# q, k and v as one long run per partition, and two small products of the attention as tiles side by side on TensorE

## The chip, the cores and the metric

The kernel runs on one core of a Trainium2 chip. TensorE multiplies, with a stationary operand of up to 128 x 128 and float32 results in PSUM; VectorE, ScalarE and GpSimd work element by element; DMA queues of SyncE (SP) and ScalarE move data between DRAM and SBUF. The metric is the device time of one execution in microseconds.

## The reference, cut to what matters

```python
def _attn_ref(q, k, v, p):                # q, k, v: 8 x 8 x 576 x 64, p: 8 x 8 x 32 x 64
    def sm_attn(qq, kk, vv):              # softmax(scale * qq kk^T) vv
        ...
    p_packed = sm_attn(p, k, v)           # p': 32 x 64 per head
    return sm_attn(q, p_packed, p_packed)

def reference(**kwargs):
    attn_out = _attn_ref(**attn_kwargs)
    x = np.ascontiguousarray(attn_out.transpose(0, 2, 1, 3)).reshape(B * S, H * D)   # 4608 x 512
    x = _moe_ref(x=x, **moe_kwargs)       # (P / Q)(x w_in) w_out, d_ff 2048
    return _moe2_ref(x=x, **moe2_kwargs)  # leaky(x w2_in) w2_out
```

The second attention ends in a product with p', and its result goes into a product with w_in. The kernel joins the two: W = p' w_in is computed once per batch (256 rows of 8 heads x 32 packed keys, 2048 columns), and the first feed-forward then multiplies the second softmax a2 with W.

## The kernel before, in words

The attention works through 16 items: item i is half a batch (4 of 8 heads), in two pairs of heads j. Eighteen units run as a software pipeline; in unit k each stage handles another item. The order inside a unit is the string `ORDER = "1AKWBwwVEWwPWQwT2WRw"`, one letter per step:

- `1` (`emit_s1`, item k): four float32 products give the scores of p and k in PSUM; VectorE takes the negated maximum `nm` (L315), ScalarE the exponential with its sum (L318).
- `T` (`emit_T`, item k-1): five transposes on TensorE (L325, L326), copied to SBUF by ScalarE and VectorE.
- `P` (`emit_PP`, item k-2): softmax times v. The 576 keys are five chunks of up to 128; each chunk is one product of 128 rows (two heads pairs x 32 packed keys, both j) with 256 columns (four heads). Of the result only the blocks of a row's own pair are used: two VectorE instructions (L344), one per half of the partitions, scale them by the sum's reciprocal and by `mask`, which zeroes the other head of the pair.
- `R` (`emit_PPT`, item k-2): p' is transposed on TensorE and copied into `pph`.
- `2` (`emit_s2`, item k-3): scores of q and p' (L361), transposed in 32 x 32 blocks by VectorE (L365), maximum (L368), subtraction on GpSimd (L369).
- `E`, `A`, `B` (items k-4, k-5): exponential on ScalarE (L372), sums, division, transpose back, and the store of a2 to DRAM, which SP issues (L389).
- `K`, `V`, `Q`: loads of k (item k+2), v (item k-1) and q (item k-2), all issued by SP; `pt`, `kt`, `vt`, `qt` are their tiles.
- `W` (`wb_step`, `emit_Wb`): one block of p' times w_in, 128 x 512, for a pair of batches bp, a pair of heads j and a quarter fc of w_in's columns; four a unit. For bp 0 `emit_Wb0` (L400) does another form, 64 x 256 products with output halves on alternating partitions, from unit 6 on; from unit 10 on `emit_Wb` (L421) runs. The stationary operand of L421 is `pph[bp][:, j]`, 128 x 128 with zeros where a head meets the other head's rows. The result lies in one of two PSUM tiles of the pool `psw`; ScalarE copies it to `wbs` (L433), in the last bp VectorE does every second one (L431). Two blocks fill a `wbs`, and `store_Wb` sends it to DRAM at the next `W`.
- `w`: one step of the work that splits float64 weights into float32 pieces, w_in until about 62 us, then half of w_out; its loads are issued by ScalarE's queue, its arithmetic stands between the attention's on ScalarE, VectorE and GpSimd.

Each engine works its list in this order, so an instruction that waits holds all behind it. After the loop the string `DRAIN` finishes the last items and ten more blocks W, the remaining six (`FILL`) stand in the first steps of the first feed-forward, which begins near 190 us.

A float32 product appears in the trace as two MATMUL records. The layout in DRAM before: q and k as [batch, pair, 128, 576], so a partition of a load gets two runs of 576 x 4 = 2304 B; v as [batch, 576, 512], so a chunk's row gives 256 x 4 = 1024 B.

## Time and profile before

| | |
|---|---|
| median of 3 runs | 1541.99 us (1541.19 to 1542.47) |
| profiled execution | 1541.61 us, its span 1539.8 us |
| TensorE (PE) busy | 1472.9 us, 96% of the span |
| VectorE (DVE) busy | 1307.6 us, 85% |
| ScalarE (ACT) busy | 1029.5 us, 67% |
| GpSimd (POOL) busy | 563.2 us, 37% |
| mean granted TensorE clock | 0.990 of 2.4 GHz |
| DMA | 322.23 MB, mean 209 GB/s |

The shares are means over stages with different limits: the attention ends near 205 us, the first feed-forward near 831 us, the second fills the rest. PEld is TensorE's loading of the stationary operand, which overlaps PE. Matmuls are pipelined, so neighbouring records overlap, and the end of a record is modelled; the chain of waits counts each stretch of time once. The DMA share is the mean busy share of 16 DMA engines; it can exceed 1 slightly.

### The profile page before, as it was taken

What the parts mean: (1) busy time and instruction counts of PE and PEld (TensorE: products, weight loads), DVE (VectorE), ACT (ScalarE), POOL (GpSimd) and SP (SyncE); (2) the same over time, 40 slices, a digit from 0 to 9 for tenths busy, and PEclk for the clock granted to TensorE, in tenths of its full rate; (3) what the DMA queues carried; (4) which work ended last, traced back from release to release, by engine and by line L of the source; (5) the groups of instructions that cost most, each with busy time, mean ns of one, the idle gap of its engine ahead of it and who ended that gap; (6) DMA issues with size and microseconds to landing.
All of it is one profiled execution on the core that took longest, in us unless ns stands there. A gap on an engine that the chain in (4) does not pass through costs nothing.

```text
span 1539.8 us, 20601 instructions
## 1 busy us (share of the span) xinstructions
PE 1472.9 (96%) x7552; PEld 1214.8 (79%) x7552; DVE 1307.6 (85%) x1428; ACT 1029.5 (67%) x1193; POOL 563.2 (37%) x338
## 2 busy tenths in 40 slices
PE   4798879999999999999999999999999999999998
PEld 2454467888888888888888877888888888888898
DVE  5989789898988998999999799968965996599586
ACT  5456488888988888888886676447534743474363
POOL 1223168788788768887664520000000000000000
PEclk9999989999999999999999999999999999999999
DMA  9798964325443533434335877997567656765694
GB/s 348 275 314 265 316 209 130 96 82 178 142 132 121 173 104 117 139 101 137 110 110 183 310 267 234 367 382 292 180 221 286 198 186 217 256 193 200 217 408 172
DMA packets 151108, 322.23 MB, mean 209 GB/s; under 512 B 14816, under 2 KB 79328, under 8 KB 149984
## 3 DMA queue, kind: packets, MB, share of 16 engines
q1 hardware_dynamic: 147552, 308.34, 58.3%
q10 hardware_dynamic: 3456, 12.58, 2.3%
q8 instruction: 60, 0.98, 0.3%
q14 instruction: 40, 0.33, 0.1%
HBM read 230.17 MB, written 90.70 MB: 208 GB/s over the span
## 4 chain that ended last, share of the span: by engine, by line
PE 55%; DVE 15%; ACT 13%; POOL 7%; issue 5%; DMA 4%; SPq 1%; ACTq 0%; POOLq 0%; DVEq 0%
PE p L1065 20%; PE p L1057 20%; PE acc L651 6%; PE h L572 4%; DVE s L91 2%; POOL s L705 2%; DMA qt<-in_qT 1%; DVE s L94 1%; DVE s L88 1%; PE pw L421 1%; PE pp L340 1%; POOL wb L522 1%; ACT h L629 1%; ACT wb L521 1%; DVE v L900 1%
## 5 line engine op out<-in xcount | busy, mean ns | idle before, releaser
L651 PE MATMUL acc<-gt,wo 128*128 128x512 f32 x1728 | 404.9, 390 | 7.0 <-ACT yo L588 7.0
L651 PEld LDWEIGHTS acc<-gt,wo 128*128 128x128 f32 x1728 | 320.1, 188 | 71.2 <-ACT yo L588 8.3
L1057 PE MATMUL p<-ysp,ws 128*128 128x512 f32 (+1 forms) x1680 | 346.9, 368 | 2.9 <-ACT vsp L985 2.4
L1065 PE MATMUL p<-vsp,ws 128*128 128x512 f32 (+1 forms) x1680 | 346.5, 368 | 0.2 <-DVE vsp L986 0.2
L1057 PEld LDWEIGHTS p<-ysp,ws 128*128 128x128 f32 x1680 | 292.5, 189 | 56.8 <-ACT vsp L985 3.4
L1065 PEld LDWEIGHTS p<-vsp,ws 128*128 128x128 f32 x1680 | 292.3, 189 | 53.7 <-DVE vsp L986 1.5
L572 PEld LDWEIGHTS h<-a2t,wb 128*128 128x128 f32 x1728 | 230.0, 194 | 30.3 <-issue 18.5
L572 PE MATMUL h<-a2t,wb 128*128 128x192 f32 (+2 forms) x1728 | 236.3, 293 | 17.3 <-DVE v__1851 L636 5.6
L985 ACT ACTIVATE vsp<-v 128x1024 fp32r<-128x1024 f32 (+1 forms) x140 | 135.7, 971 | 147.6 <-PE p L1065 98.4
L986 DVE TENSOR_TENSOR vsp<-v,vsp 128x1024 fp32r<-128x1024 f32 (+1 forms) x140 | 155.7, 1112 | 32.4 <-ACT vsp L985 31.9
L900 DVE TENSOR_TENSOR v<-v,p 128x1024 f32<-128x1024 f32 (+1 forms) x100 | 110.7, 1109 | 40.7 <-PE p L1057 40.4
L917 DVE SCALAR_TENSOR_TENSOR v<-r,nalpha,v 128x512 f32<-128x512 f32 (+1 forms) x160 | 112.3, 742 | 29.7 <-ACT v L912 29.7
L911 ACT ACTIVATE r<-v 128x1024 f32<-128x1024 f32 (+1 forms) x60 | 58.3, 972 | 76.3 <-DVE v L900 75.9
L900 DVE TENSOR_TENSOR v<-v 128x1024 f32<-128x1024 f32 (+1 forms) x80 | 88.3, 1109 | 0.0
L522 POOL TENSOR_TENSOR wb<-s,wb 128x512 fp32r<-128x512 f32 x48 | 64.7, 1348 | 31.0 <-ACT wb L521 30.5
L88 DVE TENSOR_SCALAR s<-s 128x512 f32<-128x512 f32 x48 | 63.8, 1328 | 0.6 <-ACT s L83 0.6
L912 ACT ACTIVATE v<-v 128x1024 f32<-128x1024 f32 (+1 forms) x60 | 58.6, 976 | 1.9
L91 DVE SCALAR_TENSOR_TENSOR s<-s,s 128x512 int32<-128x512 int32 x40 | 56.8, 1419 | 0.3
L925 ACT ACTIVATE v<-p 128x1024 f32<-128x1024 f32 (+1 forms) x20 | 18.9, 943 | 53.3 <-PE p L1057 53.3
L369 POOL TENSOR_TENSOR trn<-trn,mx 128x576 f32<-128x576 f32 x16 | 20.3, 1268 | 90.9 <-DVE mx L368 80.6
L900 DVE TENSOR_TENSOR c<-c,p 128x1024 f32<-128x1024 f32 (+1 forms) x25 | 27.4, 1112 | 29.9 <-PE p L1065 29.6
L421 PE MATMUL pw<-w_in,pph 128*128 128x512 f32 x96 | 48.5, 619 | 3.9 <-ACT wbs L433 3.9
(1024 smaller groups left out, 2260.6 us busy)
## 6 DMA issues: line engine op xcount, KB each, us to landing
ws<-wh_d SPq DMA_DIRECT2D x224, 512.0 KB, 5.6
wh_d<-ws SPq DMA_DIRECT2D x56, 512.0 KB, 5.0
wq_d<-s SPq DMA_DIRECT2D x32, 512.0 KB, 3.9
wst<-wq_d SPq DMA_DIRECT2D x56, 256.0 KB, 3.9
wb_d<-wbs SPq DMA_DIRECT2D x48, 256.0 KB, 4.5
s<-in_w_out SPq DMA_DIRECT2D x24, 512.0 KB, 4.4
s<-wb_d SPq DMA_DIRECT2D x48, 256.0 KB, 4.2
kt<-in_kT SPq DMA_DIRECT2D x16, 576.0 KB, 7.9
```

What stands on the lines that cost most here:

```text
L88: dve.tensor_scalar(w, w, 0.0, HIGH_R, op0=ALU.max, op1=ALU.min)
L91: dve.scalar_tensor_tensor(wi, in0=wi, scalar=3, in1=low, op0=ALU.logical_shift_left, op1=ALU.bitwise_or)
L421: mm(pw, pph[bp][:, j].rearrange("p a b -> p (a b)"), w_in_t[j, fc], start=True, stop=True)
L522: pool.tensor_tensor(t[:, 1], st, t[:, 0], op=ALU.subtract)
L572: mm(h[:, ft, o:o + m], w[x][:, k, 128 * ft:128 * ft + 128], a2_t[c][:, y, k, o:o + m], start=n == 0, stop=n == 5)
L651: mm(acc[d // 2][:, d % 2, :], w[:, x, 128 * d:128 * d + 128], t[:, y, ft, :], start=f == 0 and (x, y, ft) == (0, 0, 0), stop=f == NP - 1 ...
L900: dve.tensor_tensor(o, a, b, op=op)
L917: dve.scalar_tensor_tensor(v_[:, g], in0=r[:, g], scalar=nalpha[:, f:f + 1], in1=v_[:, g], op0=ALU.mult, op1=ALU.add)
L985: act(t[:, 0, :, 0:m], src, AF.Copy)
L986: return lambda: dve.tensor_tensor(t[:, 1, :, 0:m], src, t[:, 0, :, 0:m], op=ALU.subtract)
L1057: mm(ps[:, g, 0:m], w[:, g, x, 128 * k:128 * k + 128], ysp[s, i](z, k), start=not onto and q == 0, stop=q == 5, skip_group_check=again)
L1065: mm(ps[:, d, 0:m], w[:, g, x, 128 * d:128 * d + 128], t[:, z, g, 0:m], start=not onto and n == 0 and g == 0 and q == 0, stop=n == 3 and g ...
```

## The change

1. q and k lie in DRAM as [batch, half, 128, 2, 576]: a partition of a load is one run of 4608 B. v lies in the order of the tile: the 64 upper partitions get five chunks as one run of 5120 B, the 64 lower ones four chunks, 4096 B. The number of loads and their bytes stay.
2. Softmax times v: each chunk is two products of 64 columns of the stationary operand with 128 columns, one for each j, on output partitions 0 to 63 and 64 to 127. The result is 128 x 128 and one VectorE instruction scales and masks it; `mask` has three column blocks of 64 and is read from block 0 or 1. In pairs 1 and 2 of a batch (`TURN`) the two heads stand in turned order, which p's layout on the host sets.
3. p' times w_in: two neighbouring pairs j are computed together into two PSUM tiles by eight products of 64 rows (one head) and 32 columns (32 packed keys of one head and batch); the zero blocks are left out. The copies stay one per `W` step, in the order j0, j0+1 for a quarter of w_in's columns, then the next quarter, so two `wbs` fill at the same time.

```diff
--- before.py
+++ after.py
@@ -203,11 +203,10 @@
 
     ident = sp0.tile([128, 128], F32, tag="ident", name="ident", bufs=1)
     make_identity(nc, ident)
-    mask = sp0.tile([128, 128], F32, tag="mask", name="mask", bufs=1)
+    mask = sp0.tile([128, 3, 64], F32, tag="mask", name="mask", bufs=1)
     pool.memset(mask, 0.0)
-    for h in range(4):
-        o = 64 * (h % 2)
-        pool.memset(mask[32 * h:32 * h + 32, o:o + 64], 1.0)
+    for h, c in ((0, 0), (0, 2), (1, 1), (2, 1), (3, 0), (3, 2)):
+        pool.memset(mask[32 * h:32 * h + 32, c, :], 1.0)
 
     pt, kt, qt, vt = {}, {}, {}, {}
 
@@ -218,19 +217,18 @@
             nc.sync.dma_start(out=pt[b], in_=pT[b])
             pool.tensor_scalar(pt[b], pt[b], 0.125, None, op0=ALU.mult)
         kt[i] = sp0.tile([128, 2, S], F32, tag="kt", name="kt", bufs=3)
-        nc.sync.dma_start(out=kt[i], in_=kT[b, 2 * t:2 * t + 2].rearrange("j p s -> p j s"))
+        nc.sync.dma_start(out=kt[i], in_=kT[b, t])
 
     def load_v(i):
         b, t = divmod(i, 2)
         vt[i] = sp0.tile([128, 5, 256], F32, tag="vt", name="vt")
-        vs = v[b, :, 256 * t:256 * t + 256]
-        nc.sync.dma_start(out=vt[i][:, 0:4, :], in_=vs[0:512].rearrange("(c p) d -> p c d", p=128))
-        nc.sync.dma_start(out=vt[i][0:64, 4, :], in_=vs[512:576])
+        for r, c, x in ((0, 5, v[b, t, 0:64 * 1280]), (64, 4, v[b, t, 64 * 1280:64 * 2304])):
+            nc.sync.dma_start(out=vt[i][r:r + 64, 0:c, :], in_=x.rearrange("(p c d) -> p c d", p=64, c=c))
 
     def load_q(i):
         b, t = divmod(i, 2)
         qt[i] = sp0.tile([128, 2, S], F32, tag="qt", name="qt")
-        nc.sync.dma_start(out=qt[i], in_=qT[b, 2 * t:2 * t + 2].rearrange("j p s -> p j s"))
+        nc.sync.dma_start(out=qt[i], in_=qT[b, t])
 
     w_in_t = {}
 
@@ -333,16 +331,15 @@
     def emit_PP(i):
         pb = ps0.tile([128, 512], F32, tag="pp", name="pp")
         pps[i] = pb
-        pp = pb[:, 0:256]
+        pp = pb[:, 0:128]
         at, v_ = a1T.pop(i), vt.pop(i)
         for c in range(5):
             kc = 128 if c < 4 else 64
-            mm(pp, at[0:kc, c, :], v_[0:kc, c, :], start=c == 0, stop=c == 4)
+            for j in range(2):
+                mm(pp[64 * j:64 * j + 64, :], at[0:kc, c, 64 * j:64 * j + 64], v_[0:kc, c, 128 * j:128 * j + 128],
+                   start=c == 0, stop=c == 4)
         ppn[i] = sp0.tile([128, 128], F32, tag="ppn", name="ppn", bufs=1)
-        for j in range(2):
-            r = slice(64 * j, 64 * j + 64)
-            dve.scalar_tensor_tensor(ppn[i][r, :], in0=pp[r, 128 * j:128 * j + 128],
-                                     scalar=rs1[i][r, :], in1=mask[r, :], op0=ALU.mult, op1=ALU.mult)
+        dve.scalar_tensor_tensor(ppn[i], in0=pp, scalar=rs1[i], in1=mask[:, i % 2:i % 2 + 2, :].rearrange("p a b -> p (a b)"), op0=ALU.mult, op1=ALU.mult)
 
     def emit_PPT(i):
         b, t = divmod(i, 2)
@@ -388,7 +385,8 @@
         b, t = divmod(i, 2)
         nc.sync.dma_start(out=a2_d[b][:, t, :], in_=a2.pop(i))
 
-    wbs, stores = {}, []
+    TURN = (0, 1, 1, 0)
+    wbs, stores, pws = {}, [], {}
 
     def emit_Wb0(n):
 
@@ -409,30 +407,35 @@
         bp, r = divmod(n, 16)
         if bp == 0:
             return emit_Wb0(n)
-        j, fc = BLOCKS[r]
-        if bp == LAST and r % 4 > 1 and "ps0" in opened:
-            if fc % 2 == 0:
-                wbs[1] = ps0.tile([128, 2, 512], F32, tag="s1", name="pw")
-            pw = wbs[1][:, fc % 2, :]
-        elif bp == LAST and r % 4 > 1:
-            pw = psw2.tile([128, 512], F32, tag="wb", name="pw")
-        else:
-            pw = psw.tile([128, 512], F32, tag="wb", name="pw")
-        mm(pw, pph[bp][:, j].rearrange("p a b -> p (a b)"), w_in_t[j, fc], start=True, stop=True)
+        j0, fc = 2 * (r // 4 % 2), 2 * (r // 8) + r % 4 // 2
+        if r % 2 == 0:
+            if bp == LAST and r % 4 > 1 and "ps0" in opened:
+                two = ps0.tile([128, 2, 512], F32, tag="s1", name="pw")
+                pws[0], pws[1] = two[:, 0, :], two[:, 1, :]
+            else:
+                for x in range(2):
+                    pws[x] = (psw2 if bp == LAST and r % 4 > 1 else psw).tile([128, 512], F32, tag="wb", name="pw")
+            for q in range(4):
+                for x in range(2):
+                    bi, h = q // 2, q % 2
+                    rows, c = slice(64 * h, 64 * h + 64), 32 * (h ^ TURN[j0 + x])
+                    mm(pws[x][64 * bi + c:64 * bi + c + 32, :], pph[bp][rows, j0 + x, bi, c:c + 32],
+                       w_in_t[j0 + x, fc][rows, :], start=True, stop=True)
+        x = r % 2
         if fc % 2 == 0:
             if bp == LAST and r > 0:
-                wbs[0] = wp.tile([128, 1024], F32, tag="D", name="wbs")
-            elif bp == LAST or len(w_done) == len(w_jobs) and n % 4 == 0:
-                wbs[0] = gp.tile([128, 1024], F32, tag="s4", name="wbs", bufs=3)
+                wbs[x] = wp.tile([128, 1024], F32, tag="D", name="wbs")
+            elif bp == LAST or len(w_done) == len(w_jobs) and x == 0:
+                wbs[x] = gp.tile([128, 1024], F32, tag="s4", name="wbs", bufs=3)
             else:
-                wbs[0] = spw.tile([128, 1024], F32, tag="wbs", name="wbs")
+                wbs[x] = spw.tile([128, 1024], F32, tag="wbs", name="wbs")
         o = 512 * (fc % 2)
-        if bp == LAST and n % 2:
-            dve.tensor_copy(wbs[0][:, o:o + 512], pw)
+        if bp == LAST and x:
+            dve.tensor_copy(wbs[x][:, o:o + 512], pws[x])
         else:
-            act(wbs[0][:, o:o + 512], pw, AF.Copy)
+            act(wbs[x][:, o:o + 512], pws[x], AF.Copy)
         if fc % 2:
-            stores.append((bp, j, fc, wbs[0]))
+            stores.append((bp, j0 + x, fc, wbs[x]))
 
     def store_Wb():
         while stores:
@@ -1095,7 +1098,13 @@
     NK = p.shape[2]
 
     def pairs_T(x):
-        return np.ascontiguousarray(x.transpose(0, 1, 3, 2)).reshape(B, H // 2, 2 * D, S)
+        return np.ascontiguousarray(x.transpose(0, 1, 3, 2).reshape(B, H // 4, 2, 2 * D, S).transpose(0, 1, 3, 2, 4))
+
+    def keys_first(x):
+        x = x.reshape(B, H // 4, 4, S, D).transpose(0, 1, 3, 2, 4).reshape(B, H // 4, S, 4 * D)
+        m = x[:, :, 0:512].reshape(B, H // 4, 4, 128, 4 * D).transpose(0, 1, 3, 2, 4)
+        top = np.concatenate([m[:, :, 0:64], x[:, :, 512:576].reshape(B, H // 4, 64, 1, 4 * D)], axis=3)
+        return np.concatenate([y.reshape(B, H // 4, -1) for y in (top, m[:, :, 64:128])], axis=2)
 
     def bits(x):
         x = np.ascontiguousarray(x)
@@ -1103,11 +1112,13 @@
 
     pT = np.zeros((B, 2, D, H // 2, 2, NK), p.dtype)
     for h2 in range(2):
-        pT[:, h2, :, :, h2, :] = p[:, h2::2].transpose(0, 3, 1, 2)
+        for turn in range(2):
+            j = np.array([turn, 3 - turn])
+            pT[:, h2, :, j, h2 ^ turn, :] = p[:, 2 * j + h2].transpose(1, 0, 3, 2)
...
-        "v": np.ascontiguousarray(v.transpose(0, 2, 1, 3)).reshape(B, S, H * D),
+        "v": keys_first(v),
```

On TensorE, unit 11 of the attention (the units up to 15 are alike) was, with what each row waits for (`Activation` is ScalarE, `DVE` VectorE, `DMAHW` a landing; `ps` are the scores, `pst` the transposed softmax, `pp` softmax times v, `pw` a block of p' times w_in):

```order
L312 MATMUL ps_1081<-kt,pt 64x288 [waits DMAHW3_49,DVE_49]
L312 MATMUL ps_1081<-kt,pt 64x288 x3
L421 MATMUL pw<-w_in,pph 128x512 [waits Activation_49] x2
L340 MATMUL pp<-vt,a1T 128x256 [waits DMAHW6_49,DVE_49]
L340 MATMUL pp<-vt,a1T 128x256 x3
L340 MATMUL pp<-vt,a1T 128x256 [waits DMAHW7_49]
L421 MATMUL pw<-w_in,pph 128x512 [waits Activation_49]
L325 MATMUL pst<-ident,a_993 128x128 x4
L326 MATMUL ps_1081<-ident,a_993 64x128
L361 MATMUL ps_1155<-qt,pph 64x288 [waits DMAHW2_49]
L361 MATMUL ps_1155<-qt,pph 64x288 x3
L421 MATMUL pw<-w_in,pph 128x512 [waits Activation_49]
```

and now is:

```order
L310 MATMUL ps_1131<-kt,pt 64x288 [waits DMAHW3_49,DVE_49]
L310 MATMUL ps_1131<-kt,pt 64x288 x3
L422 MATMUL pw<-w_in,pph 32x512 [waits Activation_49]
L422 MATMUL pw<-w_in,pph 32x512 [waits PE_49,Activation_49]
L422 MATMUL pw<-w_in,pph 32x512 x6
L339 MATMUL pp<-vt,a1T 64x128 [waits DMAHW7_49,DMAHW6_49,DVE_49]
L339 MATMUL pp<-vt,a1T 64x128 x9
L422 MATMUL pw<-w_in,pph 32x512 [waits Activation_49] x2
L422 MATMUL pw<-w_in,pph 32x512 x6
L323 MATMUL pst<-ident,a_1027 128x128 x4
L324 MATMUL ps_1131<-ident,a_1027 64x128
L358 MATMUL ps_1221<-qt,pph 64x288 [waits DMAHW0_49]
```

The four blocks at four places have become two groups of eight products at the first and the third place. The first two products of each group wait for ScalarE's copies of both blocks of the group before; in the second group these copies stand on ScalarE before and behind the exponential of the second attention. No block follows the scores of q any more.

On SP, one unit of the same stretch, from the load of k to the load of q (`wb_d` is W in DRAM, `a_d` the stored a2), was:

```order
L221 DMA kt<-in_kT 128x2x576
L441 DMA wb_d_78<-wbs 64x1024
L441 DMA wb_d_79<-wbs 64x1024
L389 DMA a_d_103<-a_1093 128x576
L227 DMA vt<-in_v 128x4x256
L228 DMA vt<-in_v 64x256
L441 DMA wb_d_78<-wbs 64x1024
L441 DMA wb_d_79<-wbs 64x1024
L233 DMA qt<-in_qT 128x2x576
```

and now is:

```order
L220 DMA kt<-in_kT 128x1152
L444 DMA wb_d_78<-wbs 64x1024
L444 DMA wb_d_79<-wbs 64x1024
L386 DMA a_d_103<-a_1143 128x576
L226 DMA vt<-in_v 64x1280
L226 DMA vt<-in_v 64x1024
L231 DMA qt<-in_qT 128x1152
L444 DMA wb_d_78<-wbs 64x1024
L444 DMA wb_d_79<-wbs 64x1024
```

The load of q has moved ahead of one pair of W's stores; the loads' rows show one run per partition.

## Rows read from the trace of the kernel before

**Rows 1.** Busy time by stage: us, PE, PEld, DVE, ACT, POOL, granted clock, DMA share, GB/s
```profile
13.46:43.05 29.59, 18.58 (x80) 10.29 (x81) 23.80 (x53) 15.24 (x30) 2.85 (x3) 0.88 1.05 377
43.05:62.77 19.72, 14.55 (x65) 8.41 (x65) 16.63 (x40) 8.56 (x16) 3.68 (x2) 0.83 0.63 213
62.77:101.50 38.73, 38.73 (x259) 22.72 (x256) 35.53 (x81) 16.82 (x33) 7.72 (x7) 1.00 0.94 316
101.50:151.79 50.29, 46.21 (x200) 23.55 (x198) 44.63 (x98) 33.48 (x64) 17.60 (x15) 1.00 0.89 286
151.79:175.90 24.11, 24.11 (x94) 12.40 (x94) 18.41 (x40) 10.49 (x19) 2.95 (x3) 1.00 0.96 309
...
200.00:203.00 3.00, 1.10 (x3) 0.19 (x1) 2.93 (x5) 2.88 (x6) 0.00 (x0) 1.00 1.02 408
```

**Rows 2.** Chain of waits, first 43 us: start us, us, what
```profile
21.97 12.83 DMA qt<-in_qT
34.81 8.24 DMA qt<-in_qT
```

**Rows 3.** Chain of waits, part of a unit of the third stage
```profile
81.83 1.73 PE pw L400 x16
83.56 2.55 PE pp L340 x10
86.11 1.01 PE pw L400 x8
```

**Rows 4.** Chain of waits, a unit of the fifth stage
```profile
159.95 1.72 PE pw L421 x4
161.66 2.35 PE pp L340 x10
164.02 1.05 PE pw L421 x2
165.07 0.44 PE pst L325 x4
...
165.62 1.12 PE ps L361 x8
166.74 1.06 PE pw L421 x2
```

**Rows 5.** SP's queue, first and last of eleven loads: start us, us, issue
```profile
13.46 0.37 SPq L227 DMA_DIRECT2D vt<-in_v  x1
...
42.32 0.53 SPq L233 DMA_DIRECT2D qt<-in_qT  x1
```

**Rows 6.** Groups by line, 0 to 330 us: count, busy us, mean ns, idle before
```profile
L344 DVE SCALAR_TENSOR_TENSOR ppn<-pp,rs,mask 64x128 f32<-64x128 f32 x32 | 10.7, 334 | 2.6 <-PE pp L340 2.3
```

**Rows 7.** Timelines of VectorE, GpSimd and ScalarE, from 158.8 us: start us, us
```profile
158.83 0.85 DVE L365 STREAM_TRANSPOSE trn<-ps 128x288 f32<-128x288 f32 x2 [0.78 <-PE ps L361]
...
159.71 0.75 DVE L368 TENSOR_REDUCE mx<-trn 128x18 f32<-128x576 f32 x1
...
160.54 1.16 POOL L369 TENSOR_TENSOR trn<-trn,mx 128x576 f32<-128x576 f32 x1 [8.12 <-DVE mx L368]
...
161.73 0.68 ACT L372 ACTIVATE trn<-trn 128x576 f32<-128x576 f32 x1 [0.29 <-POOL trn L369]
162.32 0.58 ACT L433 ACTIVATE wbs<-pw 128x512 f32<-128x512 f32 x1
```

**Rows 8.** Waits, 101.5 to 151.79 us: total us, times, longest
```profile
PEld pw L421 <- ACT wbs L433: 4.6, 8, 1.5
```

**Rows 9.** Busy time of single units, columns as in rows 1
```profile
81.83:91.19 9.36, 9.36 (x67) 5.55 (x64) 8.37 (x21) 4.17 (x8) 2.01 (x3) 1.00 0.92 294
101.50:111.40 9.90, 9.90 (x43) 5.08 (x42) 8.62 (x20) 6.70 (x13) 3.29 (x3) 1.00 1.00 347
159.95:167.91 7.96, 7.96 (x33) 4.22 (x33) 6.33 (x15) 3.46 (x7) 1.16 (x1) 1.00 0.98 332
```

**Rows 10.** Timeline of GpSimd at the start
```profile
4.04 0.85 POOL L219 TENSOR_SCALAR pt<-pt 128x256 f32<-128x256 f32 x1 [1.81 <-DMA pt<-in_pT]
```

More of the change, by code (lines that the diff above doesn't have):

```diff
@@ L36, in attention_then_two_moes @@
     B = qT.shape[0]
-    S = qT.shape[3]
+    S = qT.shape[4]
     HS = S // 2
```

## The prediction

> **What bounds the kernel now.** I read the busy times by stage first, then the chain of waits inside each stage that the change touches, then single instructions for the prices. All edits lie in the attention part, which ends near 205 us. The stages behind it contain none of the edited lines; they can only start earlier or later.
>
> By stage [rows 1] the attention part has four different limits. From 13.46 to 43.05 us the DMA engines are full: share 1.05, 377 GB/s. The chain says the same [rows 2]: it hangs on landings of q of 12.83 and 8.24 us. From 43.05 to 62.77 us the DMA share falls to 0.63 and VectorE holds 16.63 of 19.72 us. From 62.77 to 101.50 us TensorE has no gap (38.73 of 38.73), with VectorE close behind (35.53) and DMA at 0.94. From 101.50 to 151.79 us VectorE (44.63 of 50.29) and ScalarE pass the work to each other, while TensorE is only nearly full. From 151.79 to 175.90 us TensorE is again without a gap and VectorE falls to 18.41.
>
> In a unit of the third stage the product of softmax and v takes 2.55 of 9.36 us [rows 3, 9]. In one of the fifth [rows 4] it takes 2.35 and the four blocks of p' times w_in take 1.72 + 1.05 + 1.06 = 3.83 of 7.96 us, all on the chain; that unit's VectorE is busy for 6.33 us [rows 9].
>
> **The change part by part.** The sum is made against the profiled execution, 1541.61 us; the median of the runs is 0.4 us above it.
>
> *Layout of q, k, v.* Runs go from 2304 B (q, k) and 1024 B (v) to 4608 B and 5120 or 4096 B; bytes and number of DMAs stay. The trace has a stretch in which almost all traffic has 4 KB runs (stores of W, parked W, w_out): 408 GB/s at share 1.02, or 400 GB/s per full share, against 377 / 1.05 = 359 in the DMA-bound stage [rows 1]. From the first to the last load shown [rows 5] SP issues, by its queue, 4 k, 4 v and 3 q loads, 11 x 0.59 MB = 6.5 MB of the stage's 377 x 29.59 = 11.2 MB. These take 6.5 / 0.377 = 17.2 us now; a tenth of that is 1.8 us, with the first loads ahead of them 2. Bounds: 0 if the limit is bytes, 4 if all traffic of the first 43 us goes at the higher rate. I take **2 us**, since both rates were measured with the queues full. Later stages are not bound by DMA, so nothing is booked there.
>
> *Softmax times v.* Five full products of 256 columns become ten of 128 columns on half the array each. The trace shows such halves in bp 0's blocks: 16 records of 256 columns in 1.73 us, 0.108 each [rows 3], where an undivided record of 512 takes 1.72 / 4 = 0.43, so 0.215 per 256 [rows 4]. Two halves therefore stream at once. Twenty records of 128 columns cost 20 x 0.054 = 1.08 us. Against 10 x 0.215 = 2.15 us of pure streaming the row of 2.55 has 0.4 for two or three changes of the array's form, 0.13 each; with one such change I take 1.25 us, which saves 1.3 us per unit in the third stage and 1.1 in the fifth.
>
> *One masked scaling instead of two.* VectorE's two instructions on 64 partitions become one on 128 with the same 128 elements per partition: at a mean of 334 ns [rows 6], 0.33 us less per unit.
>
> *Blocks of p' times w_in.* Two blocks (2 x 0.86 us) become eight products of 64 x 32 on eight different parts of the array. If all eight stream at once, the pair takes one block's 0.86 us plus a change of form on either side, 1.0 us. The trace has no quarter columns and no two row halves at once. Bounds: 0.86, and 16 records x 0.43 / 2 = 3.44 us if only two stream at once as in the nearest row. I take 1.0, because the halves of the nearest row do not disturb each other at all: each gets its full rate. This saves 1.8 us per unit from unit 10 on.
>
> *The wait that the pairs add.* A pair needs both PSUM tiles, so its first matmuls wait for both copies of the pair before, and the second of these stands on ScalarE behind the exponential of the second attention. In the fifth stage [rows 7] the loop is: transposes of VectorE end at 159.68, maximum to 160.46, GpSimd from 160.54 to 161.70, exponential to 162.41, copy to 162.9. Measured from the end of the scores (158.8) that is 4.1 us. Then follow the pair (1.0), the transposes (0.55) and the scores (1.12), with hand-overs 7.0 us a unit. Queued behind the waiting pair are the transposes of p's softmax and the next scores, for which VectorE waits.
>
> *By stage.* 13 to 43 us: 2.0. 43 to 63 us: VectorE-bound, two units at 0.33, **0.7**. 63 to 101.5 us: TensorE could save 4 x 1.3 = 5.2, but VectorE's 35.53 - 1.33 = 34.2 us, filled to 97%, needs 35.3; that leaves **3** (bounds 1.3, the scaling alone, and 4.5). 101.5 to 151.8 us: the hand-over between VectorE and ScalarE does not pass TensorE, five units at 0.33, **1.7**; the bounds are -2, if the new wait costs 0.4 a unit (TensorE's wait for these copies is 4.6 us there already [rows 8]), and 5.7, all of VectorE's idle time. 151.8 to 175.9 us: TensorE's unit of 7.96 falls by 1.1 and 1.8 to about 5.0; the loop of 7.0 and VectorE's 6.33 come next, three units at 0.9 less some ramp, **2.5** (0 to 4). 175.9 to 205.5 us: eight pairs between DMA and ScalarE waits, **0.5** (-1 to 3). SP's queue: the q load now stands ahead of a pair of W's stores, the same work in another order, nothing booked. Two more fills of the mask on GpSimd lie in the 1.81 us for which it waits for p at the start [rows 10]. Sum **10.4 us**: 1531.2, against the median about **1531.5 us**. The lowest bounds add up to about -1, the highest to 23.
>
> **Rivals.** *Row halves take turns (1534.5 us).* Products of the upper and the lower row half write to one PSUM bank, on other partitions. If such writes exclude each other, only four streams run: 16 x 0.43 / 4 = 1.72 us a pair, as now. Then the fifth and last stage gain only what v's product and the scaling give, and 7.4 us of the sum is left. For it: no row of the trace has two row halves at once. Against: halves by columns share one bank in bp 0's blocks and lose nothing [rows 3]. The Trainium skill, "TensorEngine Tiling (Array Packing)", section Restrictions and Gotchas, speaks against this edit: row tiles are to write to different banks and cannot use one bank at the same time. No run here shows it; taken at its word it is this rival.
>
> *Other limits take it all (1539.5 us).* VectorE at 92% in the third stage and the new wait in the fourth leave the scaling's 1.3 + 0.7, some DMA time and the fifth stage's first microsecond, less 2 in the fourth. A lower clock would do the same: from 43.05 to 62.77 us, with TensorE busy 14.55 of 19.72, the granted clock was 0.83 [rows 1], that is partly the 1.2 of the 1.2 and 2.4 GHz levels. Against: TensorE's work of 5 to 6.5 us a unit at 0.83 still fits in 7 to 10 us. For: VectorE's stage has only 3.2 us of gaps in four units.
>
> *Only two products at a time (1553.5 us, slower).* If the eight parts share one path for their moving columns, a pair costs 3.44 us, and TensorE's unit of the fifth stage 7.96 - 1.1 - 3.83 + 2 x 3.44 = 9.9 us: 5.8 us more over three units. In the fourth stage the scores with k, 1.12 us, come on top: 11.0 against a unit of 9.90 [rows 9], five units, 5 us. The eight last pairs cost 1.73 more each, half of it hidden, 7. Less the 6 us that loading, v's product and the scaling gain in the first 101.5 us, that is 12 us more. It decides from some 2.8 us a pair upward, i.e. when fewer than two and a half of the eight run together. For it: nothing wider than two has run in this trace. Against: the halves have shown no common limit.
>
> **How the numbers follow.** The forecast (1525 to 1537) gets 0.66; turns 0.12; other limits 0.11; two at a time 0.11. Faster, by over 0.2% (3.1 us, about what a measurement of this kernel can tell from no change): 0.66 + 0.12 + 0.02 = 0.80. Same: 0.08, most of the second rival. Slower: 0.12. The range leaves out the slow rival and the last of the upper bound: 1523 to 1543.
>
> **What would show it.** Right: v's product at 1.2 to 1.4 us per unit; the eight products within 1.1 us; q, k and v landing sooner with 380 to 395 GB/s before 43 us; units of 8.7 us near 80 and of 7 near 160; the start of the first feed-forward stage some 10 us earlier and everything after it as long as now. Wrong: a pair at 1.7 (turns) or 3.4 us (two at a time); TensorE waiting for ScalarE's copies for over 2 us a unit in the fourth stage; w_in landing so much later beside larger runs that VectorE idles before 43 us; a granted clock below 1 between 63 and 176 us.

## The result, and the profile after

The changed kernel takes **1556.5 us** (median of 4 runs, 1555.25 to 1558.99) where the kernel before takes 1541.74 beside it: a ratio of 1.0097, 95% interval 1.0083 to 1.0110, or 15 us slower. The forecast of 1531.5 us had the wrong sign. Its profiled execution took 1555.54 us, its span 1553.8; TensorE was busy for 1459.5 us, 94%, at a mean granted clock of 0.978.

Nearly all of the loss lies in the attention: the first product of the first feed-forward starts at 202.1 us instead of 189.2, that is 12.9 us later; up to the first product of the second, at 854.4 instead of 840.6, the traces differ by 0.9 us more, and from there to the end by 0.2. Inside the attention the scores of unit 11 start 1.7 us later than before (110.3 for 108.6), those of unit 15 12.9 us later (163.5 for 150.6), and behind them nothing more is lost. So 11.2 us are lost in the four units 11 to 14. The stages of rows 1, in the changed kernel (same columns):

```profile
13.46:43.05 29.59, 17.38 (x99) 9.80 (x101) 20.75 (x48) 16.53 (x31) 1.66 (x2) 0.88 1.03 337
43.05:62.77 19.72, 11.02 (x80) 6.26 (x81) 17.50 (x41) 8.59 (x16) 4.53 (x3) 0.83 0.80 247
62.77:101.50 38.73, 35.95 (x320) 21.41 (x316) 34.33 (x77) 16.68 (x32) 7.89 (x7) 0.96 0.97 317
101.50:151.79 50.29, 36.96 (x311) 14.51 (x296) 35.68 (x78) 28.02 (x53) 13.34 (x13) 0.83 0.91 273
151.79:175.90 24.11, 19.15 (x183) 7.91 (x176) 16.51 (x35) 11.63 (x22) 6.40 (x5) 0.86 0.66 202
```

Against [rows 1], three things stand out. In the DMA-bound stretch the share is about as full as before, 1.03 for 1.05, but it carries 337 GB/s instead of 377. In the fourth stage every engine does less in the same 50.29 us: TensorE 36.96 for 46.21, VectorE 35.68 for 44.63; none of them is full. And the granted clock is 0.83 there, where it was 1.00.

First the loads. The DMA view of 13.46 to 43.05 us gives the throughput in 40 slices and the median time from issue to landing of w_in's pieces (`ws`). Before:

```profile
GB/s 410 401 407 406 394 383 365 361 269 350 354 421 383 395 389 397 366 385 401 374 311 332 409 357 399 404 409 377 378 362 390 371 325 388 376 389 373 368 379 368
ws<-in_w_in ACTq DMA_DIRECT2D x9, 512.0 KB, 6.6
```

After:

```profile
GB/s 433 393 418 414 350 270 222 249 255 260 354 415 404 384 417 406 382 191 231 257 278 270 322 359 410 395 433 400 413 409 249 237 262 280 268 310 309 375 406 392
ws<-in_w_in ACTq DMA_DIRECT2D x9, 512.0 KB, 10.7
```

Three times the rate falls, mostly to 190 to 280 GB/s, for some 4 us or more and comes back. Before, a single slice of 0.74 us (269) is that low.

Then TensorE's timeline in units 11 and 12, start, duration, and in brackets the idle time with what ended it:

```profile
111.43 1.09 PE L422 MATMUL pw<-w_in,pph 64*32 64x512 f32 x16
112.61 1.46 PE L339 MATMUL pp<-vt,a1T 128*64 128x128 f32 x20
115.85 1.04 PE L422 MATMUL pw<-w_in,pph 64*32 64x512 f32 x2 [1.78 <-ACT wbs L436]
118.64 1.95 PE L422 MATMUL pw<-w_in,pph 64*32 64x512 f32 x14 [1.75 <-ACT wbs L436]
...
124.38 1.09 PE L422 MATMUL pw<-w_in,pph 64*32 64x512 f32 x16
125.40 1.46 PE L339 MATMUL pp<-vt,a1T 128*64 128x128 f32 x20
128.34 1.46 PE L422 MATMUL pw<-w_in,pph 64*32 64x512 f32 x2 [1.49 <-ACT wbs L436]
132.40 1.96 PE L422 MATMUL pw<-w_in,pph 64*32 64x512 f32 x14 [2.60 <-ACT wbs L436]
```

The tiles do nearly what was forecast: a pair's eight products (16 records) take 1.09 us, where two blocks took 1.72 in [rows 4], and softmax times v takes 1.46 us instead of 2.35 to 2.55 [rows 3, 4]. But the second pair of each unit runs in two pieces. It waits for the first copy of the pair before, writes its first product, and waits again for the second copy. On ScalarE the two copies stand here in unit 12, the first and the last row:

```profile
127.70 0.59 ACT L436 ACTIVATE wbs<-pw 128x512 f32<-128x512 f32 x1
129.56 0.63 ACT L280 ACTIVATE wo<-s 128x512 fp32r<-128x512 f32 x1 [1.27 <-DVE s L94]
130.10 0.67 ACT L369 ACTIVATE trn<-trn 128x576 f32<-128x576 f32 x1
130.67 0.65 ACT L83 ACTIVATE s<-raw 128x512 f32<-128x512 f32 x1
131.23 0.64 ACT L84 ACTIVATE raw<-raw 128x512 int32<-128x512 uint8 x1
131.77 0.57 ACT L436 ACTIVATE wbs<-pw 128x512 f32<-128x512 f32 x1
```

Between the two copies lie the exponential and three steps of w_out's splitting, the first of which waits 1.27 us for VectorE. So 4 us pass, and behind the waiting pair stand the transposes (L323, L324) and the scores of q (L358), for which VectorE then waits. The waits of 101.5 to 151.79 us (total, times, longest), to set against [rows 8]:

```profile
PEld pw L422 <- ACT wbs L436: 15.7, 8, 4.1
...
DVE a1T L328 <- PE ps L324: 5.8, 4, 1.8
DVE trn L362 <- PE ps L358: 4.2, 4, 1.8
```

TensorE's loads wait 15.7 us for the copies where they waited 4.6, and VectorE waits 10.0 for TensorE, once a unit for the last transpose and once for the scores; the same view of the kernel before lists no wait of VectorE for either. Last the clock, in neighbouring stretches:

```profile
115.20:118.60 3.40, 1.04 (x2) 0.13 (x2) 1.66 (x3) 3.38 (x8) 1.28 (x1) 1.00 0.68 232
118.60:122.00 3.40, 3.36 (x21) 1.31 (x23) 2.51 (x9) 1.33 (x3) 0.14 (x1) 0.50 0.85 234
```

In the first, TensorE was busy for 1.04 of 3.40 us and waited for the copies most of the rest; in the second the granted clock is 0.50, that is 1.2 of 2.4 GHz, while it works the held-up pair, the transposes and the scores. Units 12, 13 and 14 have such stretches too, at 0.50 from 128.80 to 135.60, from 145.90 to 149.30 and from 159.50 to 162.90 us.

### The profile page after: what moved, and what is told of

Read it like the earlier page. It is cut to its first block, busy times and chain, and to the rows that moved or that the text cites. A ratio compares the mean times of both kernels' runs of the same rounds, so it can differ in the third digit from the quotient of the medians.

```text
span 1553.8 us, 21499 instructions
## 1 busy us (share of the span) xinstructions
PE 1459.5 (94%) x8000; PEld 1198.7 (77%) x8000; DVE 1301.0 (84%) x1412; ACT 1029.9 (66%) x1193; POOL 564.8 (36%) x340
## 3 DMA queue, kind: packets, MB, share of 16 engines
q8 instruction: 64, 1.05, 0.3%
## 4 chain that ended last, share of the span: by engine, by line
PE 57%; DVE 17%; ACT 12%; POOL 5%; issue 5%; DMA 1%; SPq 0%; POOLq 0%; ACTq 0%; DVEq 0%
PE p L1068 20%; PE p L1060 20%; PE acc L654 8%; PE h L575 5%; DVE s L91 2%; POOL s L708 1%; PE pw L422 1%; DVE s L94 1%; DVE v L903 1%; DVE s L88 1%; ACT h L632 1%; DVE v L920 1%; PE ps L358 1%; DVE h L638 1%; ACT wb L524 1%
## 5 line engine op out<-in xcount | busy, mean ns | idle before, releaser
L422 PE MATMUL pw<-w_in,pph 64*32 64x512 f32 x384 | 40.0, 728 | 18.7 <-ACT wbs L436 15.0
(1024 smaller groups left out, 2231.9 us busy)
```

## The experiments

The table reads two stretches of each run. "Before 43 us" is the first row above. "Four units" is the time from the first product of the scores in unit 11 to that in unit 15, with its granted clock; the kernel before took 42.0 us at 1.00.

| run | median us | ratio to before (95%) | GB/s before 43 us | four units, clock |
|---|---|---|---|---|
| the changed kernel | 1556.5 | 1.0097 (1.0083 to 1.0110) | 337 | 53.2, 0.81 |
| 1 layout alone | 1548.98 | 1.0042 (1.0027 to 1.0057) | 313 | |
| 2 v tiles alone | 1538.41 | 0.9978 (0.9969 to 0.9988) | 376 | 41.2, 1.00 |
| 3 W tiles alone | 1552.25 | 1.0065 (1.0050 to 1.0080) | 378 | 51.6, 0.87 |
| 4 change, copies together | 1546.34 | 1.0027 (1.0017 to 1.0037) | 320 | 40.7, 0.92 |
| 5 q, k layout alone | 1541.69 | 0.9994 (0.9984 to 1.0004) | 382 | |
| 6 v halves alone | 1551.97 | 1.0063 (1.0047 to 1.0080) | 308 | |
| 7 v long runs, 128 partitions | 1542.75 | 0.9998 (0.9989 to 1.0007) | 385 | |
| 8 both tiles, old layout, copies together | 1540.65 | 0.9986 (0.9975 to 0.9996) | 376 | 42.9, 0.88 |
| 9 v halves, short runs | 1554.1 | 1.0077 (1.0063 to 1.0091) | 300 | |
| 10 pairs, full blocks | 1551.9 | 1.0066 (1.0052 to 1.0080) | 375 | 48.7, 0.93 |
| 11 change with filler | 1554.93 | 1.0082 (1.0067 to 1.0098) | 322 | 46.6, 1.00 |
| 12 order | 1539.84 | 0.9984 (0.9975 to 0.9993) | 381 | 41.3, 0.92 |
| 13 change, filler in five units | 1553.5 | 1.0069 (1.0048 to 1.0090) | 329 | 46.6, 1.00 |
| 14 as 8, with filler | 1541.23 | 0.9990 (0.9980 to 0.9999) | 378 | 41.0, 0.96 |
| 15 v tiles and q, k layout | 1536.79 | 0.9953 (0.9935 to 0.9972) | 384 | 40.3, 1.00 |

**The parts, each alone (1 to 3).** Run 1 is the kernel before with part 1 of the change, run 2 with part 2 without the turned order, run 3 with part 3.

```diff
# 1
+        nc.sync.dma_start(out=kt[i], in_=kT[b, t])
...
+        for r, c, x in ((0, 5, v[b, t, 0:64 * 1280]), (64, 4, v[b, t, 64 * 1280:64 * 2304])):
...
# 2
...
+                mm(pp[64 * j:64 * j + 64, :], at[0:kc, c, 64 * j:64 * j + 64], v_[0:kc, c, 128 * j:128 * j + 128],
...
# 3
...
+                    mm(pws[x][64 * bi + c:64 * bi + c + 32, :], pph[bp][rows, j0 + x, bi, c:c + 32],
...
```

> The kernel before with the new layout of q, k and v alone. Theory of the prediction: -2 us (1540), since the first 43 us are DMA-bound. Theory after the trace of the change: the longer runs give SP's queue more of the DMA engines and w_in, on ScalarE's queue, lands later (10.6 instead of 7.1 us), so VectorE and ScalarE wait for it: 0 to +3 us (1542 to 1545), and the first scores of unit 6 no earlier than 61.6 us.

> The kernel before with softmax times v as two column halves and one masked scaling alone. Theory (prediction): -3 to -7 us (1535 to 1539), units of 8.7 us near 80 us. Rival: TensorE, less busy, falls to 1.2 GHz in the attention and gives the gain back: within 2 us of 1541.7, with granted clock below 1 between 63 and 176 us.

> The kernel before with the paired blocks W in eight tiles alone (and p's turned order). Theory: the second group of a unit waits for the copy behind ScalarE's exponential, and TensorE, idle meanwhile, falls to 1.2 GHz: +10 to +16 us (1552 to 1558), units of 12 to 14 us between 101 and 165 us. Rival: the loss comes from the other two parts or from their sum; then this alone is within 3 us of 1541.7.

The layout costs 6.5 us (its ratio times 1542), the tiles of softmax times v gain 3.4, the W tiles cost 10. The sum of 13.1 lies at the lower end of the interval of the whole change (12.8 to 17.0), so the three parts account for it within the noise. Runs 2 and 3 came out within their expectations; the layout cost more than either theory of run 1 allowed (-2, or 0 to +3). In run 2 the chain of waits of the third stage reads

```profile
75.07 1.46 PE pp L341 x20
```

and its units there last 8.2 us (scores at 80.4, 88.6, 96.8 and 105.1) for 9.3 before. Run 1 shows the throughput dips of the changed kernel with nothing else changed; w_in's pieces land after 11.1 us.

**The copies (4).** Both copies of a pair stand directly behind its products; the rest is the changed kernel.

```diff
-        x = r % 2
+            copies(bp, r, j0, fc)
+
+    def copies(bp, r, j0, fc):
+      for x in range(2):
         if fc % 2 == 0:
-            if bp == LAST and r > 0:
+            if bp == LAST and r + x > 0:
...
```

> The changed kernel with both copies of a pair issued right behind its products, ahead of the exponential, so that the second group no longer waits for a copy behind it. Theory: the wait is the cause, with the low clock as its consequence: 1536 to 1545 us. Rival: the tiles' shorter work alone lets the clock fall, with no wait needed: 1550 us or more, and granted clock near 0.83 between 101 and 176 us as in the change.

Of the 15 us, 10.8 come back (1.0097 to 1.0027), and the four units take 40.7 us, less than before. The time, 1546.34 us, lies between the two theories (up to 1545, or 1550 and more) and nearer to the first. The second pair is no longer split; in unit 11 all its 16 records stand together behind one wait, and from 101.5 to 151.79 us TensorE's loads wait 5.4 us for copies, for 15.7 in the changed kernel and 4.6 before:

```profile
117.47 1.57 PE L422 MATMUL pw<-w_in,pph 64*32 64x512 f32 x16 [1.93 <-ACT wbs L439]
...
PEld pw L422 <- ACT wbs L439: 5.4, 7, 2.2
```

What is left, 4.2 us, is about the layout's 6.5 less what both tiles gain in run 8, 2.2. So the place of each pair's second copy on ScalarE's list makes the larger part of the loss.

**Which part of the layout (5 to 7, 9).** Run 5 has q and k alone in the new layout, run 6 v alone; run 7 gives v runs of 4096 B on all 128 partitions, and a tail on 64; run 9 leaves v's runs at 1024 B (every second KB of DRAM, by v's layout in the text ahead of the prediction, and not every fourth as its expectation has it) and cuts the loads by partition halves.

```diff
# 7
+        for r, c0, c, x in ((128, 0, 4, v[b, t, 0:128 * 1024]), (64, 4, 1, v[b, t, 128 * 1024:128 * 1024 + 64 * 256])):
+            nc.sync.dma_start(out=vt[i][0:r, c0:c0 + c, :], in_=x.rearrange("(p c d) -> p c d", p=r, c=c))
# 9
-        nc.sync.dma_start(out=vt[i][:, 0:4, :], in_=vs[0:512].rearrange("(c p) d -> p c d", p=128))
+        vp = vs[0:512].rearrange("(c p) d -> p c d", p=128)
+        nc.sync.dma_start(out=vt[i][0:64, 0:4, :], in_=vp[0:64])
...
+        nc.sync.dma_start(out=vt[i][64:128, 0:4, :], in_=vp[64:128])
```

> The kernel before with q and k alone in runs of 4608 B on 128 partitions; v is loaded as before. The whole layout cost +6.8 us in the experiment with layout alone. Theory A (what costs is v's two loads on 64 partitions each: their 5120 B packets took 347 ns against 184 ns for q's and k's of 4608 B, so they move at about half the rate and hold up the queue): this run lies within 1.5 us of the kernel before, and the first feed-forward stage begins as early as before (189.2 us). Theory B (longer runs of SyncE's queue take the share of w_in's loads, whose landing went from 7.1 to over 10 us): this run is +3 to +5 us, since q and k are two thirds of the bytes of the three.

> The kernel before with v alone in the new layout: two loads on 64 partitions, runs of 5120 and 4096 B; q and k as before. Theory A (64 partitions): +5 to +7 us, DMA throughput before 43 us near 310 GB/s as with the whole layout, ScalarE's wait for w_in's pieces twice as long as before. Theory B (run length): +1.5 to +2.5 us, a third of the bytes.

> The kernel before with v alone in another layout of long runs: one load of 4096 B runs on 128 partitions, and the last 64 keys as 1024 B runs on 64 partitions as before. Theory A: no loss, 0 to -2 us, since the long runs now reach all partitions. Theory B: +1.5 to +2.5 us, like the layout on 64 partitions. This is the run that tells run length from the number of partitions.

> The kernel before with v's runs unchanged (1024 B, every fourth KB of DRAM), but each load of v cut by partition halves: 0 to 63 and 64 to 127. If the loads on 64 partitions are what the layout costs, whatever the length of their runs, this run loses most of what v's halves in long runs lost (+9.8 us): +5 to +10 us, with about 310 GB/s at full DMA share before 43 us instead of 377. If halves cost only together with long runs, it lies within 2 us of the kernel before.

Theory A, by which the loads on 64 partitions cost, holds in its direction; theory B, by which longer runs on SyncE's queue hold back w_in, does not. Runs 5 and 7 cost nothing; runs 6 and 9 lose 9.7 and 11.9 us, more than the 5 to 7 and 5 to 10 expected. No run shows a gain or a loss by the length of the runs: v's halves lose with 5120 B and with 1024 B, and v on 128 partitions does not. Run 6 loses more than run 1, which loads v in the same way beside q and k in long runs; their intervals overlap (7.2 to 12.3 us and 4.2 to 8.8), and the difference stays unexplained. From 17.8 to 23.0 us, where the first loads of v and k pass, the windows view gives for the kernel before

```profile
17.80:23.00 5.20, 1.91 (x9) 0.83 (x5) 4.12 (x10) 3.07 (x6) 0.00 (x0) 0.97 1.06 358
```

for run 6

```profile
17.80:23.00 5.20, 2.64 (x11) 1.08 (x7) 4.50 (x10) 3.15 (x6) 0.00 (x0) 1.00 1.04 214
```

and for run 7

```profile
17.80:23.00 5.20, 1.85 (x7) 0.84 (x5) 4.09 (x9) 3.05 (x6) 0.00 (x0) 1.00 1.04 372
```

In run 9, with v's short runs in halves, a low stretch lies a little later:

```profile
23.00:28.30 5.30, 1.97 (x9) 0.98 (x9) 0.68 (x3) 3.06 (x6) 0.85 (x1) 1.00 1.09 231
```

All four show the DMA engines full. With halves they move 214 and 231 GB/s, without 358 and 372. The Trainium skill, "SBUF — State Buffer", section "Can I just issue two DMAs to hit both halves?", says that two such loads are served one after the other and that only one transfer over all 128 partitions reaches all ports. These rows agree in so far as the rate falls, to 214 from 358; that ports are the reason no run here shows. The halves from two queues were not tried.

**Wait, tiles or clock (10, 11, 13).** Run 10 keeps run 3's order of pairs and copies but computes full blocks of 128 x 512. Runs 11 and 13 are the changed kernel with ten products added behind each softmax times v, whose results nobody reads: from unit 9 on in run 11, in units 10 to 14 in run 13.

```diff
# 10
+            for x in range(2):
+                mm(pws[x], pph[bp][:, j0 + x].rearrange("p a b -> p (a b)"), w_in_t[j0 + x, fc], start=True, stop=True)
# 11 (13: if 8 <= i < 13)
+        if i >= 7:
+            for _ in range(2):
+                for c in range(5):
+                    kc = 128 if c < 4 else 64
+                    mm(pb[:, 384:512], at[0:kc, c, :], v_[0:kc, c, 0:128], start=c == 0, stop=c == 4)
```

> The experiment with W's tiles alone (1552.25 us, +10.1), but the two blocks of a pair are again full products of 128 x 512, in the new order of blocks and copies. A pair takes 1.72 us of TensorE instead of 1.0. Theory 'the added wait': the second pair still waits for the copy behind the exponential, so the loss stays, +8 to +14 us. Theory 'lower clock': the fuller array keeps the granted clock at 1 between 100 and 176 us, and the run lies at +0 to +4 us.

> The changed kernel with ten extra products of 128 x 128 (about 2.6 us of TensorE, results not read) behind softmax times v of items 7 to 15, where TensorE then waits 2.6 to 4 us for ScalarE's copy. They change neither the wait nor what it is for, only what TensorE does meanwhile. If the lower clock costs a good part of the loss: no stretch below 1 between 100 and 150 us, and 1548 to 1553 us. If the clock costs little: 1555 to 1560 us, with or without drops.

> The changed kernel with the ten extra products only in units 10 to 14 (items 8 to 12), where TensorE waits for the copies; before, they also stood in unit 9 and in the drain, where nothing waits and they cost about 3 us each time. From the start of the scores in unit 10 to those in unit 15: before 51.3 us, changed kernel 63.8, with the filler of the earlier run 56.4 at full clock. If the clock costs 7 of the 12.5 us lost there: 1548 to 1551 us in all. If the earlier gain there was an accident of that run's alignment: 1554 to 1558 us.

Run 10 loses as much as run 3, 10.2 against 10.0 us, so the small tiles are not what costs; the order of pairs and copies is. TensorE's timeline of run 10 shows the same split pair as the changed kernel:

```profile
126.45 1.12 PE L421 MATMUL pw<-w_in,pph 128*128 128x512 f32 x2
130.22 2.07 PE L421 MATMUL pw<-w_in,pph 128*128 128x512 f32 x2 [2.64 <-ACT wbs L434]
```

Runs 11 and 13 price the clock. For the four units the windows view gives for the kernel before

```profile
108.60:150.60 42.00, 37.92 (x161) 19.26 (x161) 38.03 (x83) 27.50 (x54) 15.02 (x13) 1.00 0.87 277
```

for the changed kernel

```profile
110.30:163.50 53.20, 38.28 (x297) 14.96 (x296) 36.47 (x78) 27.72 (x53) 14.89 (x12) 0.81 0.82 241
```

and for run 13

```profile
117.60:164.20 46.60, 43.41 (x377) 22.81 (x376) 36.53 (x78) 27.82 (x53) 15.49 (x12) 1.00 0.86 259
```

With more work for TensorE (43.41 us busy for 38.28) and the same for VectorE and ScalarE, these units are 6.6 us shorter; run 11 gives the same 46.6. The timelines show where. In unit 11 of the changed kernel the held-up pair goes on 8.33 us after the unit's start, at 118.64 us, and the next unit starts here:

```profile
123.26 1.19 PE L310 MATMUL ps<-kt,pt 128*64 128x288 f32 x8
```

That is 4.62 us for the rest of the pair, the transposes and the scores of q, most of it at the lower clock. In run 13 unit 11 reads

```profile
117.59 1.19 PE L310 MATMUL ps<-kt,pt 128*64 128x288 f32 x8
...
125.93 1.09 PE L427 MATMUL pw<-w_in,pph 64*32 64x512 f32 x14 [0.76 <-ACT wbs L441]
...
129.02 1.19 PE L310 MATMUL ps<-kt,pt 128*64 128x288 f32 x8
```

that is 8.34 us up to the same place and 3.09 behind it. Over the four units the stretch ahead of that place takes 34.0 us in the changed kernel and 34.3 in run 13, the stretch behind it 19.2 and 12.4. So the filler leaves the wait as it is, and what it saves lies in work that TensorE does at the full clock instead of the lower one. Of the 11.2 us by which the four units grew from 42.0, the lower clock costs 6.6, and 4.6 are left for the wait at full clock.

As a change the filler is worth little, 1.6 us in run 11 and 3.0 in run 13 by the medians. Run 13 was expected at 1548 to 1551 us if the clock costs 7 us there, at 1554 to 1558 if not, and came out between, at 1553.5: its unit 10 took 15.7 us, for 10.6 in the changed kernel, because v landed late and the first filler met the lower clock:

```profile
107.32 2.60 PE L339 MATMUL pp<-vt,a1T 128*64 128x128 f32 x20 [3.09 <-DMA vt<-in_v]
109.85 4.71 PE L345 MATMUL pp<-vt,a1T 128*128 128x128 f32 x20
```

The filler took 4.71 us there, for 3.08 in each of the four units. By the scores of unit 15 run 13 stands at 164.2 us, the changed kernel at 163.5. Run 11, at 1554.93, also lies between its two forecasts (up to 1553, or 1555 and more). The two causes are not independent: run 4, where that wait is short, still has stretches of lower clock (0.92 in all), yet its four units are no longer than before. That fits a clock that is dear only where the held-up work already stands on the path.

**What the W tiles are worth without the wait (8, 12, 14).** Run 8 is run 4 with the layout of before. Run 12 has also the second pair behind the scores of q, and q and k in long runs; run 14 is run 8 with five filler products in units 10 to 15.

```diff
# 12
-    ORDER = "1AKWBwwVEWwPWQwT2WRw"
+    ORDER = "1AKWBwwVEWQwPwT2WWRw"
# 14
+        if 8 <= i < 14:
+            for _ in range(1):
...
```

> The changed kernel with the layout of before, and with both copies of a pair of W blocks right behind its products. If the parts add up (whole change with copies together +4.2 us, layout +6.8): 1542.17 + 4.2 - 6.8 = about 1539.5 us, range 1537 to 1542, still not below the kernel before with the tiles for softmax times v alone (1538.4). The theory that W's tiles would pay once nothing waits gives 1534 or less. The theory that the lower clock is what they cost expects stretches of granted clock 0.5 between 100 and 176 us, which the tiles for softmax times v alone did not have.

> The kernel with both kinds of tiles, the old layout of v, q and k in one run of 4608 B, both copies of a pair right behind its products, and the second pair of a unit behind the scores of q instead of ahead of the transposes, so that what it waits for holds back neither the transposes nor the scores. If that wait and what stands behind it is all that keeps W's tiles from paying: 1530 to 1536 us, below the tiles for softmax times v alone (1538.4). If VectorE's and ScalarE's work sets the units, the tiles give nothing: 1537 to 1541 us.

> The kernel with both kinds of tiles, the old layout and both copies right behind a pair's products (1540.65 us, five stretches of lower clock between 100 and 176 us), with five extra products of 128 x 128 (1.3 us, results not read) in units 10 to 15. If the lower clock is what keeps W's tiles from paying once the wait is gone: no lower clock there and 1534 to 1538 us. If VectorE and ScalarE set the units: 1539 to 1543 us, with or without a lower clock.

All three lie at 1540 to 1541 us, with intervals that overlap run 2's (1538.4), and their four units take 41.0 to 42.9 us against run 2's 41.2. So with a freer TensorE they are not clearly shorter than with the tiles for v alone. Run 14, at a clock of 0.96 for run 8's 0.88, has four units 1.9 us shorter than run 8 and no shorter time in all. That is what the expectations forecast if VectorE and ScalarE set the pace there, and in unit 11 of run 12 TensorE waits for VectorE:

```profile
116.49 0.47 PE L349 MATMUL pp<-ident,ppn 128*128 128x128 f32 x1 [3.62 <-DVE rs L328]
```

A run with less work for VectorE in these units, which would settle it, was not made. In the fifth stage, run 8's scores of q start here:

```profile
147.06 1.19 PE L359 MATMUL ps<-qt,pph 128*64 128x288 f32 x8
...
154.41 1.19 PE L359 MATMUL ps<-qt,pph 128*64 128x288 f32 x8
...
161.28 1.19 PE L359 MATMUL ps<-qt,pph 128*64 128x288 f32 x8
```

Units of 7.35 and 6.87 us, as forecast for it (7.0), for 7.96 before [rows 9]. That gain only makes up for a later start: the first of these rows stands at 143.6 us in run 2, 3.5 us earlier, and the first feed-forward starts at 184.2 us in run 8 and at 183.7 in run 2. From 175.90 to 205.50 us run 8 has a clock of 0.76, run 2 of 0.91; whether that takes a further gain away was not tried apart.

**The parts that did not lose (15).** Run 2 with q and k in the new layout.

```diff
-        nc.sync.dma_start(out=kt[i], in_=kT[b, 2 * t:2 * t + 2].rearrange("j p s -> p j s"))
+        nc.sync.dma_start(out=kt[i], in_=kT[b, t])
...
-        nc.sync.dma_start(out=qt[i], in_=qT[b, 2 * t:2 * t + 2].rearrange("j p s -> p j s"))
+        nc.sync.dma_start(out=qt[i], in_=qT[b, t])
```

> The two parts that did not lose, together: the kernel before with the tiles for softmax times v (1538.4 us) and with q and k in one run of 4608 B per partition (-0.9 alone, within its interval). If they add up: 1537 to 1538.5 us.

1536.79 us beside 1542.15: 5.4 us faster by the medians, 0.47% (0.28 to 0.65) by the ratio, the best version here, and a little below the 1537 to 1538.5 us expected. Its interval meets that of run 2, so the share of q and k is not settled.

## Why the prediction was wrong

*The bound now* was read rightly: four stages with different limits, and everything after 205 us as long as it was.

*Layout, forecast 2 us of gain, bounds 0 to 4.* This step failed, and with its sign. It priced the length of a run by a stretch at 408 GB/s [rows 1], whose loads and stores differ in more than that, and bounded the term below at nothing without a row that excluded a loss. Length turned out to be worth nothing measurable (runs 5, 7). The edit changed another thing on the way, the number of partitions that one load of v covers, which the text on the change shows and the prediction did not price. They cost about 10 us alone, and 6.5 with q's and k's new layout. The sign that the prediction named for being wrong here, w_in landing later and VectorE idling, is what appeared (10.7 us for 6.6, VectorE busy for 20.75 us for 23.80), though not by larger runs.

*Softmax times v.* The mechanism holds; the size was 1.46 instead of 1.25 us. The units near 80 us fell to 8.2 us (forecast 8.7). From the scores of unit 6 to those of unit 11 run 2 saves 3.6 us, for a forecast of 3 in that stage; in the fourth stage it saves 0.8 in four units, about half of the 1.7. In all the part gave 3.4 us.

*Blocks of W.* A pair took 1.09 us, forecast 1.0, with all eight products at once. Both rivals on the tiles fall: not 1.72 (turns), not 3.44 (two at a time). The rule of the Trainium skill weighed there ("TensorEngine Tiling (Array Packing)", Restrictions and Gotchas), by which row halves cannot use one bank at the same time, did not show in this pair's 1.09 us: the measurement decides.

*The wait that the pairs add.* This step failed most. The place was right (a copy behind the exponential, the transposes and scores queued behind the pair), but its length was worked out only for the fifth stage, where ScalarE has little else [rows 7]. For the fourth it was put at 0 with a bound of 0.4 us a unit, from a view of TensorE's weight loads [rows 8] and the argument that VectorE's and ScalarE's hand-over does not pass TensorE. It does once the pair holds the transposes and the scores. In the fourth stage the exponential stands among w_out's splitting, so the two copies are 4 us apart, and TensorE stood still for 3.5 us in unit 11 and 4.1 in unit 12. With the lower clock that came with it, it cost 11.2 us in four units, where the bound allowed 0.4 us a unit. Undoing that one thing gave 10.8 us back (run 4).

*The clock* appeared only inside a rival, at 0.83, as something that TensorE's shorter units could bear. With the wait it cost 6.6 us in four units (runs 11, 13); with a short wait the units are no longer than before at 0.92 (run 4).

*The slower case* of the prediction needed a pair of 2.8 us or more. The change became slower by another way, the added wait, which entered only the rival of other limits, at 2 us in the fourth stage. Three of the signs of being wrong did name what came: TensorE waiting for copies, w_in landing later, and a granted clock below 1 between 63 and 176 us. The highest bounds of the sum add up to 21.9 us and not 23; nothing in the account hangs on it.

## What to carry to other kernels

Before a load is repacked for longer runs, count the partitions that each DMA covers before and after, and read GB/s beside the DMA share: here a full share of 1.04 went with 214 GB/s and with 372. When two results are grouped so that their work needs both buffers at once, look up where the last release of each stands in its engine's list, in the stage where that engine is fullest, and put the releases right behind the group. Run each part of a change alone: here one part gained 3.4 us, and two others that were to gain as well lost 6.5 and 10.

## What was not expected of the hardware

- With v's loads cut into partition halves, all DMA traffic of a stretch ran at 214 GB/s with the DMA engines full at a share of 1.04 (run 6), where it ran at 358 at 1.06 with whole loads. With 1024 B runs in halves a stretch ran at 231 GB/s at 1.09 (run 9).
- Eight products of 64 x 32 wrote two PSUM tiles, upper and lower row halves of the array into one tile on other partitions, in 1.09 us for 16 records of 512 columns.
- TensorE was busy for 1.04 us from 115.20 to 118.60 us, and from 118.60 to 122.00 the granted clock was 0.50; products whose results nobody reads, put into such waits, kept it at 1.00 and made four units 6.6 us shorter.
